# A Fourier mixing layer and windowed attention on one core: sums of v for six blocks a visit, T 19 blocks behind S

## The chip, the cores and the metric

The kernel runs on one core of one Trainium2 chip. A core has TensorE (PE in the profile; its weight loads are PEld), VectorE (DVE), ScalarE (ACT), GpSimd (POOL) and SyncE (SP), which here issues nearly all DMAs. The metric is the device time in microseconds of one execution; lower is better.

## The reference, cut to what matters

One input x of 2048 positions and 512 features goes through two branches, and a gate mixes them:

```
a = x @ Dre.T ; b = x @ Dim.T            # transform along the features
A = Cre @ a - Cim @ b                    # transform along the sequence, 2048 x 2048
q, k, v = x @ wqkv                       # 32 heads of 16
p = softmax(q k^T / 4), over the last 256 positions
B = (p v) @ wo
g = sigmoid(sum(x * gate_w))
out = g * A + (1 - g) * B
```

Products with float32 accuracy are made of three products of halves: each operand is split into a rounded high part (hi) and the rest (lo), and PE does hi hi, hi lo and lo hi.

## The kernel before, in words

**Two kinds of work side by side.** PE's order is written out by hand: the main loop at the end of the function issues, for each step n, the attention work of a few blocks and between them `fill(n)`, which takes the next matmuls out of a generator, `dense()`. The other engines' orders come from a scheduler that simulates times, with some instructions pinned behind others (`behind`, `late`). So a change in the loop can move instructions on every engine.

**Attention.** A block is 64 positions of one group of 8 heads, handled as four pairs p; there are 4 groups with 32 blocks, N = 128. Its way has two passes over the scores.
- S (`s_pair`, L355): the scores of a block as rows, four matmuls `s`. DVE adds the mask and takes the extreme of each row (L357), ACT the exponentials and their sum (L360). Eight blocks later `ml_split`, `ml_turn` and `ml_rows` turn these numbers into rows, which go through DRAM into four spare rows of `ring[0]` (`m_ring`, at n = 8u + 12).
- T (`t_pair`, L438): LAG = 18 blocks behind S, the scores again, transposed, with the m rows in the product. ACT writes the exponentials to `pt` (L439), POOL clears the corners (L444, L448). T of block 8u - 4 is the first that reads the m rows of u, because a block reaches 320 positions ahead.
- Sums of v (`pv`, L465): matmuls 32 columns wide, four beside each other on PE. They are done for several blocks in one go, a visit, once enough blocks have their exponentials: three blocks, and five when `more` isn't empty, that is, when the projections are through and only the sequence transform is left to fill in. The buffers for the exponentials are four of the pool, and from then on two more in `home`, a tile that held the outgoing projections.
- `o_out` (L486) multiplies a finished tile by the reciprocals of the sums and stores it to `o_scr`.

**Dense work.** `dense()` yields, in order: q, k and v of the first group (L270, L293), the other groups' q and k, the transform along the features (dab, L293), and then the sequence transform (dc, L517) in pieces: a piece is 128 x 1024 weights of Cre or Cim. Each is loaded to `raw` (two buffers, L94), split by DVE to hi and lo (L569, in `split_soon`: four jobs, taken at every sixth matmul), and used by 24 matmuls. `Pieces.get` takes a piece, starts the split of the next one and the load of the one after it. hi and lo come from a pool with three buffers each. `c_half` does half a sum of one output block; its accumulator r is loaded from `r_scr` when it starts and added when it is done (`ended`, taken at the second matmul of the next stretch).

**The end.** When the attention is through, `attention_done` loads wo through the same `raw` buffers and splits it (`fin`); for each output block, `wo_prep` loads o from `o_scr` and splits it on ACT and DVE (`os`, L78, L81), and `wo_block` multiplies (L777). These stand between the last pieces of dc.

**Queues.** SP issues in order; a DMA that waits holds all behind it. The last lines of `s_pair` and others record their instruction (`mark`), so that a pinned one can be put behind them.

Of the kernel before, what the change touches and what calls it, by code (L numbers as in the profile page):

```python
# [7 lines left out]
F32 = mybir.dt.float32  # L8
F32R = mybir.dt.float32r
AF = mybir.ActivationFunctionType  # L10
OP = mybir.AluOpType
# [11 lines left out]
WIN = 320  # L23
BIG = 1e30
SCALE = 0.25
LAG = 18
WARM = 8
SWITCH = 6
FILL_FIRST, FILL_PROJ, FILL_SEQ = 3.0, 4.0, 3.7
# [3 lines left out]
def fnet_window_mix(ctx: ExitStack, tc: tile.TileContext, xT, x, wqk, wv, wr, wi, cr, ci, wo, gw, out):  # L33
# [24 lines left out]
    def f(ap):  # L58
        return ap.bitcast(F32)
# [4 lines left out]
    def mark(e, ins):  # L64
        last[e] = ins.ins

    @contextmanager
    def behind(*engines):
        with ExitStack() as es:
            for e in engines:  # L70
                if e in last:
                    es.enter_context(tc.issue_after(last[e]))
            yield
# [15 lines left out]

    HALVES = slice(0, 512), slice(512, 1024)  # L90

    def load_raw(src):
        raw = st.tile([P, 1024], F32, name="raw", bufs=2)
        ld(raw, src)  # L94
        return raw

    def split_raw(raw, act=False):
        hi = st.tile([P, 1024], F32R, name="hi")
        lo = st.tile([P, 1024], F32R, name="lo")
        for c in HALVES:  # L100
            split(hi[:, c], lo[:, c], raw[:, c], act)
        return hi, lo
# [2 lines left out]
    ended = []  # L105

    def split_soon(raw):
        hi = st.tile([P, 1024], F32R, name="hi")
        lo = st.tile([P, 1024], F32R, name="lo")
        for c in HALVES:  # L110
            jobs.append(lambda c=c: late(nc.vector.tensor_copy, hi[:, c], raw[:, c]))
            jobs.append(lambda c=c: late(nc.vector.tensor_sub, lo[:, c], raw[:, c], f(hi[:, c])))
        return hi, lo
# [27 lines left out]

    with tc.manual_schedule(engines={mybir.EngineType.Activation, mybir.EngineType.DVE, mybir.EngineType.SP}):
        wraw, *xraw = [pt_raw() for _ in range(3)]
        wq0 = [st.tile([P, 1024], F32R, name=h) for h in ("hi", "lo")]
        zero = ev.tile([P, 512], F32R, name="ev")
        nc.vector.memset(f(zero[:]), 0.0)
        for dk in (0, 2, 1, 3):
            XRAW[dk, 0] = xraw[dk // 2][:, HALVES[dk % 2]]
            if dk % 2 == 0:
                nc.scalar.dma_start(XRAW[dk, 0], xT[0, dk])  # L150
        for dk in range(DK):
            ld(wraw[:, dk * 256:dk * 256 + 256], wqk[0][:, dk * 256:dk * 256 + 256])
            if dk % 2 == 0:
                ld(XRAW[dk + 1, 0], xT[0, dk + 1])
        for dk in range(DK):
            c = slice(dk * 256, dk * 256 + 256)
            mark("act", nc.scalar.copy(wq0[0][:, c], wraw[:, c]))
            split_x(0, (dk,), dk > 0)
            mark("dve", nc.vector.tensor_sub(wq0[1][:, c], wraw[:, c], f(wq0[0][:, c])))
# [27 lines left out]
                                        base=e - 1, channel_multiplier=-1)  # L187

    def clear_rows(i, ss):
        nc.gpsimd.memset(f(ring[i][96:128, :, ss * 512:(ss + 1) * 512]), 0.0)  # L190

    first_lo = f(XT[0, 0][96:128, 1]).rearrange("r (p c) -> r p c", p=NP)
    for t in pads[0]:
        nc.gpsimd.affine_select(t[96:128], first_lo, pattern=[[0, NP], [0, P]], compare_op=OP.is_gt, fill=0.0,
                                base=0, channel_multiplier=0)
    clear_rows(1, 0)
    clear_rows(0, 0)
    vpad = [const.tile([P, 4, NP, 32], F32, name=f"vpad{b}") for b in range(2)]
# [38 lines left out]
    TERMS = ((0, 0), (0, 1), (1, 0))  # L237


    home = const.tile([P, 3072], F32R, name="home")  # L240
    turn = iter(range(99))

    def hl_tile():
        c = next(turn) % 3 * 1024
        return home[:, c:c + 1024].rearrange("p (h s) -> p h s", h=2)

    def qk_evict(g, ss, i, ps):
        hl = hl_tile()
# [149 lines left out]
    OT = {}  # L398
    V2 = {}
    PT = {}  # L400
    more = []

    VR = {}
# [21 lines left out]
    def t_pair(n, p):  # L425
        q0 = n % NB * BQ
        w = min(WIN, S - q0)
        if p == 0:
            if "proj" in have:
                more.append(n)  # L430
            c = (n - more[0]) % 6 * NP * WIN if more else 3072
            if c + NP * WIN <= 3072:
                PT[n] = f(home[:, c:c + NP * WIN].rearrange("p (a b) -> p a b", a=NP))
            else:
                PT[n] = at.tile([P, NP, WIN], F32, name="pt", bufs=4)
        pt = PT[n]
        ps = ps_a.tile([P, 512], F32, name="t", tag="st")
        nc.tensor.matmul(ps[:, :w], PAD[1, n][:, p], ring[0][:, p, q0:q0 + w], start=True, stop=True)  # L438
        nc.scalar.activation(pt[:, p, :w], ps[:, :w], AF.Exp, scale=-1.0)  # L439
        if p % 2:  # L440
            ph = slice(p - 1, p + 1)
            for h in (0, 64):
                a = pt[h:h + 64, ph, 0:64]
                nc.gpsimd.affine_select(a, a, pattern=[[0, 2], [1, 64]], compare_op=OP.is_ge, fill=0.0,  # L444
                                        base=0, channel_multiplier=-1)
                if w == WIN:
                    a = pt[h:h + 64, ph, 256:320]
                    nc.gpsimd.affine_select(a, a, pattern=[[0, 2], [-1, 64]], compare_op=OP.is_gt, fill=0.0,  # L448
                                            base=0, channel_multiplier=1)
# [97 lines left out]
            dma.dma_start(out[15][:, c], r[:, c])  # L547
        yield

    def c_half(get, half, tb, j, ab, done, after=None):  # L550
        ps = ps_d.tile([P, 512], F32, name="dc", tag="d")
        w = get((half, tb * 2 + j))
        r = done[0](tb)
        for c in range(2):
            if after:
                after()
            k = 8 * j + 4 * c
            yield from c_part(w, range(16)[k:k + 4], ab, ps, (8 * j, 8 * j + 7))
            if c == 0:
                yield  # L560
        ended.append(lambda: late(done[1], tb, ps, r))
        yield
# [13 lines left out]
    def dense():  # L576
# [128 lines left out]
        for j in range(2):  # L705
            for tb in lasts:
                yield from c_half(pieces.get, 0, tb, j, ab,
                                  (lambda t: None, lambda t, ps, r: store_r(t, ps)) if j == 0 else
                                  add(lambda t: r_scr[0][t], lambda t: r_scr[2][t]),
                                  next_b if j else None)  # L710
        ab = nxt
        wait = []

# [16 lines left out]
        for j in range(2):  # L730
            for tb in first:
                yield from c_half(pieces.get, 1, tb, j, ab, add(r_in, lambda t: r_scr[2][t]) if j == 0 else
                                  add(lambda t: r_scr[2][t], lambda t: r_scr[1][t], wait.append),
                                  None if j else next_b)
        for tb in range(SWITCH, 16):
            if tb in O:
                mixed[tb] = wo_block(tb, 0)
            for w in [w for w in wait if w in O]:
                wait.remove(w)
                ld(out[w], wo_block(w, 1))  # L740
            if FIN and tb < 15:
                for w in (tb + 1, *wait[:-(-len(wait) // (15 - tb))]):
                    wo_prep(w)
            yield from c_block(pieces.get, 1, tb, ab, add_r) if tb < 15 else c_final(pieces.get, ab, mixed.pop(15))
# [82 lines left out]

    for n in range(N + LAG + 1):
        if n in (1, 3, 5):
            for i in range(2):  # L830
                clear_rows(1 - i, (n + 1) // 2)
        if n == 7:
            clear_pads()
        k = n - LAG
        ring_ahead(n + 1)
        if k in (-1, 4):
            v_spread(0 if k < 0 else 4)
        if k in (-4, -1, 4):
            v_next({-4: 0, -1: 4, 4: 8}[k])
        if n == 0:  # L840
            make_pad(0, 0)
        for p in range(NP):
            if n < N:
                s_pair(n, p)
            fill(n)
            if 0 <= k < N:
                t_pair(k, p)
            if p == 0:
                make_pad(0, n + 1)
                if k >= -1:  # L850
                    make_pad(1, k + 1)
            fill(n)
            for at_n, at_p, do in TURN:
                u, j = divmod(n - at_n, 8)
                if p == at_p and j == 0 and 0 <= u < 16:
                    do(u)
            if p == 3 and k % 8 == 6 and 0 <= k < N:
                l_load(k // 8)
            if p == 0 and full:
                o_out()  # L860
            if p == 2 and (k - summed >= (5 if more else 3) or k == N):
                for j in range(summed, k):
                    pv(j)
                summed = k
            if p == 3 and 4 * spread - 5 < summed and 4 * spread < N and n >= fresh:
                v_spread(4 * spread)
                spread += 1
                v_next(4 * spread)
                fresh = n + 2
# [49 lines left out]
```

## Time and profile before

| | |
|---|---|
| median of 3 runs | 859.54 us (859.01 to 862.26) |
| profiled execution | 859.55 us |
| its span, first to last instruction | 857.4 us |
| granted TensorE clock | 1.000 |
| DMA moved | 160.50 MB, mean 187 GB/s |
| POOL's selects on `pt` (L444, mean) | 357 ns |
| S exponentials on ACT (L360, mean) | 542 ns |
| S mask and extreme on DVE (L357, mean) | 463 ns |

The time of an execution is 2.15 us more than the span of its instructions. Matmuls overlap on PE: a 128 x 512 matmul is shown with 395 ns, while the next one starts about 230 ns after it; what one costs is read from start to start.

### The profile page before, as it was taken

What the parts mean: (1) busy time and instruction counts of PE and PEld (TensorE: products, weight loads), DVE (VectorE), ACT (ScalarE), POOL (GpSimd) and SP (SyncE); (2) the same over time, 40 slices, a digit from 0 to 9 for tenths busy, and PEclk for the clock granted to TensorE, in tenths of its full rate; (3) what the DMA queues carried; (4) which work ended last, traced back from release to release, by engine and by line L of the source; (5) the groups of instructions that cost most, each with busy time, mean ns of one, the idle gap of its engine ahead of it and who ended that gap; (6) DMA issues with size and microseconds to landing.
All of it is one profiled execution on the core that took longest, in us unless ns stands there. A gap on an engine that the chain in (4) does not pass through costs nothing.

```text
span 857.4 us, 17208 instructions
## 1 busy us (share of the span) xinstructions
PE 849.5 (99%) x5166; PEld 690.4 (81%) x5166; DVE 621.6 (72%) x2011; ACT 588.0 (69%) x1793; POOL 371.7 (43%) x1067
## 2 busy tenths in 40 slices
PE   9999999999999999999999999999999999999998
PEld 7888787887887888887788878888877888878887
DVE  5688977777978788777788777898878844455541
ACT  5488888888888888777888887786777654401110
POOL 9200344545533545555545564553456666510000
PEclk9999999999999999999999999999999999999999
DMA  7876678484857173536264546897963544247652
GB/s 252 287 221 202 193 255 260 164 283 167 253 184 215 37 228 116 161 116 166 90 175 130 152 135 210 262 284 247 253 205 120 200 149 142 99 147 247 209 172 98
DMA packets 94573, 160.50 MB, mean 187 GB/s; under 512 B 27280, under 2 KB 36240, under 8 KB 94480
## 3 DMA queue, kind: packets, MB, share of 16 engines
q1 hardware_dynamic: 94048, 158.76, 59.3%
q8 instruction: 40, 0.66, 0.3%
q10 hardware_dynamic: 432, 0.66, 0.2%
q14 instruction: 53, 0.43, 0.2%
HBM read 108.00 MB, written 51.38 MB: 186 GB/s over the span
## 4 chain that ended last, share of the span: by engine, by line
PE 96%; DVE 2%; DMA 1%; issue 0%; ACT 0%; SPq 0%; DVEq 0%
PE dc L517 40%; PE dab L293 10%; PE s L355 9%; PE dqk L270 9%; PE t L438 8%; PE o L465 8%; PE dv L293 5%; PE t L777 5%; DMA ring<-m_scr 1%; PE s L258 1%; DVE sm L357 1%; DVE pad L338 0%; DMA pt<-xT 0%; DVE lo L569 0%; PE s L375 0%
## 5 line engine op out<-in xcount | busy, mean ns | idle before, releaser
L517 PE MATMUL dc<-big,hi 128*128 128x512 f32 x1020 | 350.3, 395 | 0.0
L360 ACT ACTIVATE sm<-sm,ml 128x320 f32<-128x320 f32 (+4 forms) x512 | 277.1, 542 | 92.1 <-DVE ml L357 87.0
L357 DVE CUSTOM_DVE_ANT_0 sm<-s,mask 128x320 f32<-128x320 f32 (+4 forms) x512 | 234.7, 463 | 106.3 <-PE s L355 78.5
L444 POOL TENSOR_SCALAR_AFFINE_SELECT pt<-pt 64x128 f32<-64x128 f32 x392 | 140.1, 357 | 222.6 <-ACT pt L439 211.9
L517 PEld LDWEIGHTS dc<-big,hi 128*128 128x128 f32 x1020 | 183.3, 188 | 26.7 <-issue 1.1
L517 PE MATMUL dc<-big,lo 128*128 128x512 f32 x510 | 201.4, 395 | 0.0
L439 ACT ACTIVATE pt<-t 128x320 f32<-128x320 f32 (+4 forms) x392 | 160.6, 410 | 48.5 <-PE t L438 46.0
L355 PE MATMUL s<-ring,pad 128*128 128x320 f32 (+4 forms) x512 | 158.6, 310 | 0.6 <-DVE ml L357 0.4
L438 PE MATMUL t<-ring,pad 128*128 128x320 f32 (+4 forms) x512 | 154.6, 302 | 1.8 <-DMA ring<-m_scr 1.6
L338 DVE TENSOR_SCALAR pad<-ring,half 96x256 fp32r<-96x256 f32 x384 | 120.0, 360 | 19.0 <-PE t L438 18.6
L355 PEld LDWEIGHTS s<-ring,pad 128*128 128x128 f32 x512 | 96.1, 188 | 34.0 <-issue 9.5
L448 POOL TENSOR_SCALAR_AFFINE_SELECT pt<-pt 64x128 f32<-64x128 f32 x344 | 116.1, 337 | 0.0
L438 PEld LDWEIGHTS t<-ring,pad 128*128 128x128 f32 x512 | 96.1, 188 | 23.8 <-ACT sm L360 2.0
L517 PEld LDWEIGHTS dc<-big,lo 128*128 128x128 f32 x510 | 95.9, 188 | 13.4 <-issue 0.5
L569 DVE TENSOR_TENSOR lo<-raw,hi 128x512 fp32r<-128x512 f32 x142 | 97.9, 699 | 0.0
L360 ACT ACTIVATION_READ_ACCUMULATOR sm<-sm,ml 128x1 f32 x512 | 97.4, 190 | 0.0
L293 PE MATMUL dab<-hi,big 128*128 128x512 f32 x256 | 89.2, 394 | 0.0
L270 PE MATMUL dqk<-big,hi 128*128 128x512 f32 x240 | 84.9, 393 | 0.0
L569 DVE CAST hi<-raw 128x512 fp32r<-128x512 f32 x142 | 61.9, 447 | 16.9 <-PE dc L517 15.8
L444 POOL TENSOR_SCALAR_AFFINE_SELECT home<-home 64x128 f32<-64x128 f32 x120 | 45.7, 381 | 61.4 <-ACT home L439 54.2
L422 POOL COPY vpad<-vr 64x256 f32<-64x256 f32 x64 | 26.5, 414 | 103.4 <-DMA vr<-v_scr 74.2
L336 ACT ACTIVATE pad<-ring,half 96x256 fp32r<-96x256 f32 x128 | 63.8, 499 | 0.0
(96 smaller groups left out, 958.3 us busy)
## 6 DMA issues: line engine op xcount, KB each, us to landing
qk_scr<-home SPq DMA_DIRECT2D x32, 512.0 KB
ring<-qk_scr SPq DMA_DIRECT2D x32, 512.0 KB
raw<-cr SPq DMA_DIRECT2D x32, 512.0 KB
raw<-ci SPq DMA_DIRECT2D x32, 512.0 KB
r_scr<-ev SPq DMA_DIRECT2D x41, 256.0 KB
ev<-r_scr SPq DMA_DIRECT2D x41, 256.0 KB
ab_scr<-home SPq DMA_DIRECT2D x20, 512.0 KB
big<-ab_scr SPq DMA_DIRECT2D x20, 512.0 KB
```

The source lines that it names most:

```text
L270: nc.tensor.matmul(ps, w[a][:, c:c + 128], XT[dk, ss][:, b], start=n == 0, stop=n == 11)
L293: nc.tensor.matmul(ps, XT[dk, ss][:, a, c * 128:(c + 1) * 128], wh[b], start=n == 0, stop=n == 11)
L338: nc.vector.tensor_scalar(dst, src, half[:96, h:h + 1], None, op0=OP.mult)
L355: nc.tensor.matmul(ps[:, :w], PAD[0, n][:, p], ring[1][:, p, k0:k0 + w], start=True, stop=True)
L357: mark("dve", nc.vector.tensor_tensor_reduce(out=sm[:, :w], in0=ps[:, :w], in1=mask[:, WIN - w:], scale=1.0, scalar=3e38, op0=OP.add, op1= ...
L360: mark("act", nc.scalar.activation(sm[:, :w], sm[:, :w], AF.Exp, bias=nm[:, c], scale=-1.0, accum_out=l[:, c]))
L438: nc.tensor.matmul(ps[:, :w], PAD[1, n][:, p], ring[0][:, p, q0:q0 + w], start=True, stop=True)
L439: nc.scalar.activation(pt[:, p, :w], ps[:, :w], AF.Exp, scale=-1.0)
L444: nc.gpsimd.affine_select(a, a, pattern=[[0, 2], [1, 64]], compare_op=OP.is_ge, fill=0.0, base=0, channel_multiplier=-1)
L448: nc.gpsimd.affine_select(a, a, pattern=[[0, 2], [-1, 64]], compare_op=OP.is_gt, fill=0.0, base=0, channel_multiplier=1)
L517: nc.tensor.matmul(ps, w[a][:, i % 8 * 128:i % 8 * 128 + 128], ab[SC[i]][:, b], start=i == ends[0] and a + b == 0, stop=i == ends[1] and a ...
L569: return fn(*args)
```

## The change: what it does

- **Visits.** With `more`, the sums wait for six blocks instead of five, and stop at an even block.
- **Buffers of exponentials.** Eight instead of six from then on: four of the pool, four in a new view of `home`, which grows from 3072 to 5120 columns.
- **Weights.** hi and lo no longer come from a pool of three. There are three fixed pairs; the first lies in the first 2048 columns of `home`, and the order of use is written out. The first ten weights go round the three pairs as before; all later ones, the pieces of the sequence transform, use the other two in turn. That frees the columns of `home` for exponentials.
- **LAG** is 19.
- **Accumulators.** `c_half` may load r for the following half in the middle of its own (`ahead`).
- **The end.** Once `FIN` is set, ended sums are added ahead of the next block's output products.
- POOL's clears of the ring rows are pinned behind its first selects.

The diff, cut to its core:

```
-LAG = 18
+LAG = 19
...
+    home = const.tile([P, 5120], F32R, name="home")
+    slots = iter([0, 1, 2] * 3 + [0] + [1, 2] * 32)
+    hls = [[const.tile([P, 1024], F32R, name=f"{h}{i}") for h in ("hi", "lo")] for i in range(2)]
+    hls.insert(0, [home[:, c] for c in (slice(0, 1024), slice(1024, 2048))])
+
+    def wslot():
+        return hls[next(slots)]
...
     def split_soon(raw):
-        hi = st.tile([P, 1024], F32R, name="hi")
-        lo = st.tile([P, 1024], F32R, name="lo")
+        hi, lo = wslot()
...
-        nc.gpsimd.memset(f(ring[i][96:128, :, ss * 512:(ss + 1) * 512]), 0.0)
+        with behind("pool"):
+            nc.gpsimd.memset(f(ring[i][96:128, :, ss * 512:(ss + 1) * 512]), 0.0)
...
-        return home[:, c:c + 1024].rearrange("p (h s) -> p h s", h=2)
+        return home[:, 2048 + c:3072 + c].rearrange("p (h s) -> p h s", h=2)
...
-            c = (n - more[0]) % 6 * NP * WIN if more else 3072
-            if c + NP * WIN <= 3072:
-                PT[n] = f(home[:, c:c + NP * WIN].rearrange("p (a b) -> p a b", a=NP))
+            if len(more) == 1:
+                PTS.append(const.tile([P, 4, NP, WIN], F32, name="pts", tag="home"))
+            c = (n - more[0]) % 8 if more else 4
+            if c < 4:
+                PT[n] = PTS[0][:, c]
...
-    def c_half(get, half, tb, j, ab, done, after=None):
+    def c_half(get, half, tb, j, ab, done, after=None, after_tb=None):
...
-        r = done[0](tb)
+        r = ahead.pop(0) if ahead else done[0](tb)
...
             if c == 0:
+                if after_tb is not None:
+                    ahead.append(done[0](after_tb))
                 yield
...
         for tb in range(SWITCH, 16):
+            if FIN:
+                while ended:
+                    ended.pop(0)()
...
-            if p == 2 and (k - summed >= (5 if more else 3) or k == N):
-                for j in range(summed, k):
+            if p == 2 and (k - summed >= (6 if more else 3) or k == N):
+                end = k - k % 2 if more else k
+                for j in range(summed, end):
                     pv(j)
-                summed = k
+                summed = end
```

More of the change, by code (lines that the diff above doesn't have):

```diff
@@ L107, in split_soon @@
     def split_soon(raw):
-        hi = st.tile([P, 1024], F32R, name="hi")
-        lo = st.tile([P, 1024], F32R, name="lo")
+        hi, lo = wslot()
         for c in HALVES:
@@ L143, in fnet_window_mix @@
         wraw, *xraw = [pt_raw() for _ in range(3)]
-        wq0 = [st.tile([P, 1024], F32R, name=h) for h in ("hi", "lo")]
+        wq0 = wslot()
         zero = ev.tile([P, 512], F32R, name="ev")
@@ L189, in clear_rows @@
     def clear_rows(i, ss):
-        nc.gpsimd.memset(f(ring[i][96:128, :, ss * 512:(ss + 1) * 512]), 0.0)
+        with behind("pool"):
+            nc.gpsimd.memset(f(ring[i][96:128, :, ss * 512:(ss + 1) * 512]), 0.0)
     first_lo = f(XT[0, 0][96:128, 1]).rearrange("r (p c) -> r p c", p=NP)
     for t in pads[0]:
-        nc.gpsimd.affine_select(t[96:128], first_lo, pattern=[[0, NP], [0, P]], compare_op=OP.is_gt, fill=0.0,
-                                base=0, channel_multiplier=0)
+        mark("pool", nc.gpsimd.affine_select(t[96:128], first_lo, pattern=[[0, NP], [0, P]], compare_op=OP.is_gt,
+                                             fill=0.0, base=0, channel_multiplier=0))
     clear_rows(1, 0)
@@ L237, in fnet_window_mix @@
     TERMS = ((0, 0), (0, 1), (1, 0))
-    home = const.tile([P, 3072], F32R, name="home")
     turn = iter(range(99))
@@ L400, in fnet_window_mix @@
     PT = {}
+    PTS = []
     more = []
@@ L548, in c_final @@
         yield
-    def c_half(get, half, tb, j, ab, done, after=None):
+    ahead = []
+    def c_half(get, half, tb, j, ab, done, after=None, after_tb=None):
         ps = ps_d.tile([P, 512], F32, name="dc", tag="d")
         w = get((half, tb * 2 + j))
-        r = done[0](tb)
+        r = ahead.pop(0) if ahead else done[0](tb)
         for c in range(2):
@@ L709, in dense @@
                                   add(lambda t: r_scr[0][t], lambda t: r_scr[2][t]),
-                                  next_b if j else None)
+                                  next_b if j else None, tb + 1 if j and tb < 15 else None)
         ab = nxt
@@ L733, in dense @@
                                   add(lambda t: r_scr[2][t], lambda t: r_scr[1][t], wait.append),
-                                  None if j else next_b)
+                                  None if j else next_b, tb + 1 if tb + 1 < SWITCH else None)
         for tb in range(SWITCH, 16):
+            if FIN:
+                while ended:
+                    ended.pop(0)()
             if tb in O:
```

## The prediction

> **What bounds the kernel now.** I read the page first, then who waited for whom on PE, then the chain that ended last.
>
> ```profile
> span 857.4 us, 17208 instructions
> ...
> PE 849.5 (99%) x5166; PEld 690.4 (81%) x5166; DVE 621.6 (72%) x2011; ACT 588.0 (69%) x1793; POOL 371.7 (43%) x1067
> ...
> PE 96%; DVE 2%; DMA 1%; issue 0%; ACT 0%; SPq 0%; DVEq 0%
> ```
>
> PE is busy for 99% of the span and holds 96% of the chain. Its work isn't changed: the same matmuls run in another order. So only three things can move the time: what PE waits for, what it loses between matmuls of different kinds, and new waits.
>
> ```profile
> PE t L438 <- DMA ring<-m_scr: 1.6, 1, 1.6
> PE dv L574 <- DVE ev L146: 1.5, 1, 1.5
> PE s L258 <- DVE big L80: 0.5, 1, 0.5
> PE s L355 <- DVE ml L357: 0.4, 2, 0.2
> ```
>
> These are all of PE's waits: 4.0 us. The second and third are the start, which the change leaves alone. The first is a single stall of 1.6 us, a T matmul that waits for the m rows.
>
> **Sums of v: three visits fewer.** The chain in order of time has each visit of L465 as one row: start, length, count of matmuls.
>
> ```profile
> 163.08 1.75 PE o L465 x24
> ...
> 552.35 2.84 PE o L465 x56
> ...
> 791.21 10.88 PE dc L517 x48
> ```
>
> The first row is a visit of three whole blocks, the second one of five. A block costs (2.84 - 1.75) / 2 = 0.545 us, so 1.75 - 3 x 0.545 = 0.115 us of a visit belongs to no block. The third row gives a dc matmul alone: 10.88 / 48 = 0.227 us. Around the second visit the timeline of PE has more:
>
> ```profile
> 551.57 0.31 PE L438 MATMUL t<-ring,pad 128*128 128x320 f32 x1
> 551.72 0.63 PE L517 MATMUL dc<-big,hi 128*128 128x512 f32 x2
> 552.28 1.28 PE L465 MATMUL o<-home,vpad 128*32 128x320 f32 x16
> 553.38 1.81 PE L465 MATMUL o<-pt,vpad 128*32 128x320 f32 x40
> 555.12 0.41 PE L355 MATMUL s<-ring,pad 128*128 128x320 f32 x1
> 555.37 0.39 PE L517 MATMUL dc<-big,lo 128*128 128x512 f32 x1
> ```
>
> Two dc matmuls at 0.23 would end at 552.18, and L465 starts at 552.28: 0.10 us lost on the way in. On the way out the s matmul takes 0.25 us to the next start (555.12 to 555.37), where the t matmul ahead of the visit took 0.15 (551.57 to 551.72): 0.10 lost again. A visit so costs 0.10 + 0.115 + 0.10 = 0.32 us beside its blocks.
>
> Visits before: 12 of three blocks up to block 36, 18 of five up to 126, one of two: 31. After: 12, 15 of six, one of two: 28; the instruction order of the changed kernel has these 28. The gain is 3 x 0.32 = **0.96 us**. A six-block visit lasts about 0.115 + 6 x 0.545 = 3.4 us. No new wait lies in it: its last block's exponentials are used some 5 x 0.545 = 2.7 us after it begins. The even limit keeps the end of one output tile and the first use of the tile after next out of one visit, so o_out always gets in between.
>
> **T one block later: the stall on the m rows.** The stall, and the issue of the load:
>
> ```profile
> 617.18 0.66 SPq L56 DMA_DIRECT2D ring<-m_scr  x1
> ...
> 621.79 0.63 PE L517 MATMUL dc<-big,hi 128*128 128x512 f32 x2
> ...
> 624.04 0.39 PE L438 MATMUL t<-ring,pad 128*128 128x320 f32 x1 [1.62 <-DMA ring<-m_scr]
> ```
>
> Two dc matmuls and then t should be 0.46 us apart; they are 2.25: **1.79 us** lost. The rows came 6.9 us after their issue. With LAG 19 this T block stands one block later while m_ring keeps its place at block 8u + 12. How long is a block?
>
> ```profile
> 529.40:552.30 22.90, 22.90 (x118) 19.43 (x117) 21.16 (x70) 19.76 (x62) 13.46 (x40) 1.00 0.64 212
> ...
> 634.50:658.10 23.60, 23.54 (x121) 19.59 (x124) 22.33 (x76) 20.03 (x64) 14.39 (x40) 1.00 0.46 155
> ```
>
> These are windows between two visits, five blocks each (length; then PE, PEld, DVE, ACT, POOL busy). A block is 4.6 us. The rows were 1.8 us late and get 4.6 us more, so I count the whole 1.79 as gained. In the new order the load of v for a later group stands directly ahead of this m load on SP's queue, and it waits for POOL; that wait would have to cost 2.8 us more than before. Kept ends: 0 and 1.79.
>
> **Weights in two slots instead of three.** Each split then waits for the matmuls of the piece before. While S runs, the split is issued after the third matmul of the next piece, when those are done: no wait is added, and in the new order no split has a wait on PE of its own until S has ended. After that DVE does stand for PE. Behind it stand the pads of T, and each still has over 4 us of PE work between that release and its first use. I count nothing; the work that covers it is DVE's slack, 23.60 - 22.33 = 1.3 us in the fullest window above, and if that goes PE stands. The run between visits is now six blocks at the same load, so the short s waits (0.4 us above) may grow or go: ends -1 and +1 us, taken as 0, the nearest row. The earlier ev loads, the fixed order of POOL's clears and the eight buffers get nothing: no row above has PE waiting for any of them.
>
> **The end: the first output product comes sooner.** The loop has one block more, so it uses 11 more dc matmuls, and they are missing as cover behind the last sums.
>
> ```profile
> 762.39 0.54 PE L465 MATMUL o<-pt,vpad 128*32 128x128 f32 x16
> 762.86 0.74 PE L517 MATMUL dc<-big,hi 128*128 128x512 f32 x2
> ...
> 777.32 4.97 PE L777 MATMUL t<-fin,os 128*128 128x512 f32 x21
> ```
> ```profile
> 754.04 8.59 SPq L56 DMA_DIRECT2D raw<-wo  x2
> 763.51 0.33 SPq L56 DMA_DIRECT2D raw<-ci  x1
> 764.12 0.33 SPq L56 DMA_DIRECT2D o_scr<-ev  x1
> ...
> 769.33 2.58 SPq L56 DMA_DIRECT2D ev<-o_scr  x5
> ```
> ```profile
> 763.41 0.68 DVE L486 TENSOR_TENSOR ev<-o,ev 128x512 f32<-128x512 f32 x1
> 765.91 0.76 DVE L80 CAST fin<-raw 128x512 fp32r<-128x512 f32 x2 [1.82 <-DMA raw<-wo]
> 766.59 1.29 DVE L81 TENSOR_TENSOR fin<-raw,fin 128x512 fp32r<-128x512 f32 x2
> 768.74 0.76 DVE L569 CAST hi<-raw 128x512 fp32r<-128x512 f32 x2 [0.86 <-DMA raw<-ci]
> ...
> 773.36 0.69 DVE L81 TENSOR_TENSOR os<-ev,os 128x512 fp32r<-128x512 f32 x1 [2.66 <-ACT os L78]
> ```
> ```profile
> 772.71 0.62 ACT L78 CAST os<-ev 128x512 fp32r<-128x512 f32 x1 [13.03 <-DMA ev<-o_scr]
> ```
>
> Let v be the end of the last sums (762.86). Before, L777 came at v + 14.5 and its first os was whole at v + 11.2 (774.05). In the new order 52 dc matmuls stand there: PE arrives at v + 52 x 0.227 = v + 11.8.
>
> The chain is longer now. The first wo load waits for a split that waits for the end of a piece on PE. Behind that end stand 12 dc matmuls and three narrow t (2.9 us) and the visit (762.39 to 762.86, 0.47), so it lies at v - 3.4; with a subtraction of 0.7 and SP's step the load goes out at v - 2.5. A load of this size took 3.6 us (the second wo: issued in the last 0.33 us before 754.04 + 8.59 = 762.63, used at 765.91): v + 1.1. Fin's first half, 2.0 us (765.91 to 767.88): v + 3.1. L486, which now stands behind it on DVE, 0.7: v + 3.8; store of o, 0.1 later. The store took 5.2 us (764.12 to 769.33) behind two such loads; behind one I take 4.2: v + 8.1. Load of o, 3.4 (769.33 to 772.71): v + 11.5. ACT and DVE, 1.35 (772.71 to 774.05): v + 12.85. The first two matmuls of L777 (0.45 us) don't need DVE's half. So PE stands 12.85 - 0.45 - 11.8 = **0.6 us**. With 5.2 us for the first load and for the store it is 3.2; with none of DVE's new order in the way, 0.
>
> The Trainium skill (DMA: Bandwidth & Descriptors, "Anatomy of one DMA") fits a DMA by 2.0 us plus its bytes at 436 GB/s, measured on another issue path; 256 KB would be 2.6 us by it, an estimate. By that rule the store and the load of o save 2.4 us, the stall is gone and the sum is 856.8. The trace has 5.2 and 3.4, and I go by these.
>
> **Sum.** The profiled execution took 859.55 us, against a median of 859.54. 859.55 - 0.96 - 1.79 + 0.6 = **857.4 us**.
>
> **Rivals.**
> - *The m rows are late again.* The v load ahead of them holds SP, and the stall stays: 859.55 - 0.96 + 0.6 = 859.2. For it: two vr loads stood near that m load before as well. Against it: 4.6 us more room. Chance 0.12.
> - *Slower: the end.* Fin, then the product, then the store, all behind a late wo load: 3.2 us instead of 0.6, which gives 860.0. It decides from 2.75 us on, when both gains are spent. For it: a ci load took 5.2 us (763.51 to 768.74). Against it: one large load fewer ahead of the store. Chance 0.12.
> - *Slower by more: DVE.* With 95% busy in the fullest window, a wait of 0.2 us on the slot in each of some 40 pieces beside S would come through to PE: 857.4 + 8 = 865. Against it: the order puts the split behind the release. Chance 0.08.
> - *Faster: short stalls go too.* The gaps too short for the list of waits shrink by some 2 us, as DVE's bursts and T's fall on other blocks, and the end costs nothing: 854.8. Chance 0.08.
> - *Buffers were the bubble.* Each visit's 0.32 us would be a wait for a free buffer, and eight buffers end it: 859.55 - 31 x 0.32 - 1.79 + 0.6 = 848.4. Against it: the loss is the same for visits of three and five, and PE's list has no such wait. Chance 0.03. The Trainium skill (Perfetto Trace Analysis, "Optimization Strategy") says that a gap that repeats on the saturated engine can mean too few buffers; the rows here don't bear that out.
>
> That the visits don't become larger is excluded by the order of the instructions.
>
> **How the numbers follow.** The forecast has the remaining 0.57. It and the first two rivals (0.81 together) give the range: down to 859.55 - 2.75 - 1 with a little for scatter, 855.0; up to 860.0 plus 1 us of s waits, 861.3 with scatter. Half a per cent is 4.3 us, about what a measurement of this kernel can tell from no change. Faster by more: the last two rivals, 0.11. Slower by more: DVE, 0.08. Within: 0.81.
>
> **What would show it.** Right: 28 runs of the sums on PE, six blocks in about 3.4 us; no wait of t for the m rows; at the first output product a wait of PE for os of under 1.5 us. Wrong: a wait of that kind over 2.7 us; s matmuls that wait for DVE in sum over 2 us; a split of weights beside S that waits for dc; an in-visit loss that isn't near 0.32.

## The result and the profile after

The changed kernel takes **863.66 us** (median of 16 runs, 862.57 to 866.16) against 860.06 for the kernel before in the same series: a ratio of 1.0041 (95% interval 1.0028 to 1.0054). It is slower by 3.6 us; I had forecast 2.1 us less. The profiled execution has a span of 861.7 us, 4.3 more than before. These are the lines of its page that answer to those of before:

```profile
span 861.7 us, 17211 instructions
...
PE 853.9 (99%) x5166; PEld 692.0 (80%) x5166; DVE 620.8 (72%) x2011; ACT 588.6 (68%) x1793; POOL 372.7 (43%) x1067
...
PE 95%; DVE 2%; DMA 2%; issue 1%; ACT 1%; SPq 0%; DVEq 0%; ACTq 0%
```

PE has the same 5166 matmuls and is busy 4.4 us longer (853.9 against 849.5). All of the loss is in there. The list of PE's waits (total, times, longest) has nothing of that size:

```profile
PE dv L587 <- DVE ev L152: 1.5, 1, 1.5
PE s L361 <- DVE ml L363: 1.3, 3, 0.9
PE s L264 <- DVE big L80: 0.4, 1, 0.4
PE t L447 <- DVE mhl L392: 0.4, 1, 0.4
PE s L264 <- DVE big L81: 0.3, 1, 0.3
PE s L361 <- ACT pts L448: 0.3, 1, 0.3
```

In sum it is 4.2 us against 4.0. The wait for the m rows is gone, as forecast, and none for the output products has come; in its place s waits 1.3 us for DVE, which was 0.4. The chain in order of time (start, length) shows what the list can't:

```profile
550.20 3.38 PE o L474 x64
...
795.23 10.99 PE dc L526 x48
```

The first is a visit of six blocks, 3.38 us long as forecast (3.4). The second is the row that stood at 791.21 before, 48 dc matmuls and nothing between them: 10.99 us instead of 10.88. The work is the same and PE waits for nothing, and each matmul takes 0.229 us instead of 0.227. Only 2.3 ns, but there are 3,758 matmuls outside the sums.

So I took the start times of all matmuls from both traces and split the time from each start to the next: 0.4427 ns per column (226.7 ns for 512) as the ideal; up to 60 ns above it as loss of spacing; more than that as a stall; the visits of the sums by themselves (their ideal is a quarter of 0.4427 ns per column, as four stand beside each other).

| us | before | after | difference |
|---|---|---|---|
| ideal | 748.8 | 748.8 | 0 |
| loss of spacing | 15.55 | 20.38 | **+4.82** |
| stalls over 60 ns, the m rows | 1.79 | 0 | -1.79 |
| other stalls over 60 ns | 13.84 | 15.82 | +1.98 |
| visits, over their ideal | 38.36 | 37.66 | -0.70 |

The sum is +4.3, the difference of the spans. The table tells how the time is divided, not why. Of the 4.82 us, 3.0 stand where a long matmul is followed by a short s or t (2.71 us before, 5.73 after, at some 990 places), 1.3 between two long ones (dv, dqk and dab; from dc to dc it went from 4.46 to 4.21), 0.5 behind short ones. So the row of dc matmuls is a sign of the loss and not where most of it stands. The granted clock is 1.00 in both profiles. What also changed are addresses: the 36 KB of `home` and the weight pairs now lie first in SBUF, and everything else has moved.

### The profile page after: what moved, and what is told of

The parts are those of the page before. It is cut to its first block, busy times and chain, and to the rows that moved or that the text cites. A ratio compares the mean times of both kernels' runs of the same rounds, so it can differ in the third digit from the quotient of the medians.

```text
span 861.7 us, 17211 instructions
## 1 busy us (share of the span) xinstructions
PE 853.9 (99%) x5166; PEld 692.0 (80%) x5166; DVE 620.8 (72%) x2011; ACT 588.6 (68%) x1793; POOL 372.7 (43%) x1067
## 4 chain that ended last, share of the span: by engine, by line
PE 95%; DVE 2%; DMA 2%; issue 1%; ACT 1%; SPq 0%; DVEq 0%; ACTq 0%
PE dc L526 40%; PE dab L299 10%; PE dqk L276 9%; PE s L361 9%; PE o L474 8%; PE t L447 8%; PE dv L299 5%; PE t L793 5%; DMA qk_scr<-home 1%; DMA pt<-wqk 1%; DVE pad L344 1%; PE s L264 0%; DVE sm L363 0%; PE s L381 0%; DVE lo L582 0%
## 5 line engine op out<-in xcount | busy, mean ns | idle before, releaser
L453 POOL TENSOR_SCALAR_AFFINE_SELECT pt<-pt 64x128 f32<-64x128 f32 x332 | 119.4, 360 | 196.5 <-ACT pt L448 184.4
L448 ACT ACTIVATE pt<-t 128x320 f32<-128x320 f32 (+4 forms) x332 | 135.1, 409 | 37.7 <-PE t L447 35.2
L453 POOL TENSOR_SCALAR_AFFINE_SELECT pts<-pts 64x128 f32<-64x128 f32 x180 | 69.8, 388 | 83.3 <-ACT pts L448 76.4
L366 ACT ACTIVATION_READ_ACCUMULATOR sm<-sm,ml 128x1 f32 x512 | 97.6, 191 | 0.0
L448 ACT ACTIVATE pts<-t 128x320 f32<-128x320 f32 (+1 forms) x180 | 74.0, 413 | 32.9 <-PE t L447 28.8
L582 DVE TENSOR_TENSOR lo<-raw,hi 128x512 fp32r<-128x512 f32 x136 | 94.4, 696 | 1.8
L457 POOL TENSOR_SCALAR_AFFINE_SELECT pt<-pt 64x128 f32<-64x128 f32 x280 | 93.8, 335 | 0.0
L582 DVE CAST hi<-raw 128x512 fp32r<-128x512 f32 x136 | 59.6, 440 | 31.4 <-PE dc L526 27.9
L276 PE MATMUL dqk<-big,home 128*128 128x512 f32 x264 | 76.8, 396 | 0.0
L299 PE MATMUL dab<-hi,big 128*128 128x512 f32 x192 | 70.3, 398 | 0.1
```

Source lines behind the costliest of these rows:

```text
L276: nc.tensor.matmul(ps, w[a][:, c:c + 128], XT[dk, ss][:, b], start=n == 0, stop=n == 11)
L299: nc.tensor.matmul(ps, XT[dk, ss][:, a, c * 128:(c + 1) * 128], wh[b], start=n == 0, stop=n == 11)
L366: mark("act", nc.scalar.activation(sm[:, :w], sm[:, :w], AF.Exp, bias=nm[:, c], scale=-1.0, accum_out=l[:, c]))
L582: return fn(*args)
```

## The experiments

Theory **place**: where the operands lie in SBUF sets the spacing. Rival **order**: the new order of work, the two slots and the waits cost the 3.6 us. Addresses below are bytes per partition, as the compiled kernels have them.

**e1: a map of places.** A kernel of matmuls alone.

> This kernel computes none of the reference: 45 tiles of 4 KB per partition fill SBUF with zeros, and TensorE alone runs 128x512 matmuls with the weights and the moving data at chosen pairs of tiles (a grid of 12 x 12 places, 8 matmuls each, then finer steps, then the hi-hi, hi-lo, lo-hi pattern of the sequence transform). Nothing else runs beside them. Theory 'place' (the spacing of matmuls depends on where the two operands lie in SBUF): the mean spacing differs from cell to cell, from about 226 ns to 229, 232 or more, and is constant within a cell. Rival 'order' (the extra 4.8 us between matmuls of the changed kernel comes from its order of work and its waits): every cell has the same spacing, 226.5 ns within 0.5. If place holds, the grid also tells which relation counts: weights below the moving data, or one of the operands in the low part of SBUF.

All 144 cells of the grid, from 1 KB to 181 KB for either operand, have 226.6 or 226.7 ns. So "low" and "high" mean nothing by themselves. But 71 of the 72 cells with finer steps had means of 230 to 234 ns, at every place alike, with a pattern set by the steps' size. They have only eight matmuls each, so the change from cell to cell is in them too (see e9). Place held in another form than I had it: the region doesn't count, and the low bits of the addresses were the next suspect.

**e2 to e4: the same instructions at other places.** The order on every engine is that of the kernel they come from; only the order of the pools differs. e2:

```
 big = tile_pool("big", bufs=16)
+wt = tile_pool("wt", bufs=1)
-home = const.tile([P, 5120] ...)      # the pairs and pts likewise
+home = wt.tile([P, 5120] ...)
```

> The changed kernel with the same instructions in the same order on every engine; only the pool of the weights (home and the two pairs) is opened behind that of the 16 big tiles, so that the pairs lie at 167104 to 183487 as they did before, above the moving data, and pads and rings lie where they did before. Theory 'place': the spacing in the quiet end goes from about 229 back to 226.5 ns, the small excess between matmuls from 20.4 to about 15.5 us, and the time from 863.7 to about 858.8 us (span near 857), a little under the kernel before. Rival 'order': nothing changes, 863.7 us, 229 ns.

In e3 `wt` is opened between const and big:

> As the run before it, but the weights lie between the rings and the big tiles (pairs at 101568 to 117951, big at 117952 to 183487 as in the changed kernel). Theory 'place' with 'weights below the moving data' as the relation: as slow as the changed kernel, 863.7 us, 229 ns in the quiet end. Theory 'place' with 'an operand in the low 80 KB' as the relation: about 858.8 us, 226.5 ns. Rival 'order': 863.7 us.

In e4, the kernel before, hi and lo come from a pool opened ahead of const:

> The kernel before with the same instructions in the same order on every engine; only the pool of the three pairs of weights is opened first, so that they lie at 1152 to 25727, and everything that lay below them moves up by 24576 bytes. Theory 'place': about 4.8 us slower, near 864.9 us, with 229 ns in the quiet end. Rival 'order': 860.1 us as before, 226.5 ns.

e2: **858.62 us**, ratio to before 0.9974 (0.9961 to 0.9987). e3: **858.82**, 0.9978 (0.9967 to 0.9989). e4: **864.30**, 1.0047 (1.0029 to 1.0064). The rows of 48 dc matmuls, in the chains of e2, e3 and e4:

```profile
792.31 10.88 PE dc L526 x48
```
```profile
790.77 10.88 PE dc L526 x48
```
```profile
795.08 10.99 PE dc L517 x48
```

The rival falls: with not one instruction moved, the changed kernel gains 5 us, and the kernel before loses 4. The loss of spacing goes with it: 15.27, 14.73 and 19.28 us. e3 also rules out "weights below the moving data".

**e5: which bits.** In the compiled addresses the weights and the big tiles differ by a multiple of 128 bytes before and in e2 and e3, and by an odd multiple of 64 after and in e4.

> This kernel computes none of the reference: TensorE alone runs cells of 40 matmuls of 128x512 (zeros), each cell with one offset of the weights and one of the moving data within their tiles (0, 32, 64, 96, 128 bytes each, then some of 8 and 16, then cells whose matmuls alternate between two pairs of offsets, then 128x320); both tiles begin at a multiple of 128 bytes. Theory 'halves' (a matmul is slow where its weights and its moving data begin in different 64-byte halves of a 128-byte unit): 226.7 ns where both offsets are 0, both 64 or 128 against 0; about 229 ns in the mean where one is 0 and the other 64. Rival 'low' (an operand in the low part of SBUF makes it slow): all cells alike, since all lie at 1 to 9 KB. Rival 'odd starts' (any start that is no multiple of 128 bytes costs by itself): 64 against 64 is slow too.

Windows of 32 spacings each (length, then busy times of PE and PEld; the counts include matmuls cut by the edges; the 1.00 behind them is the granted clock), with weights and moving data at 0 and 0, 0 and 64, 0 and 128, 64 and 0, 64 and 64:

```profile
15.71:22.97 7.26, 7.26 (x34) 6.01 (x32) 0.00 (x0) 0.00 (x0) 1.00 0.01 2
34.14:41.47 7.33, 7.33 (x34) 6.01 (x32) 0.00 (x0) 0.00 (x0) 1.00 0.00 0
52.66:60.13 7.47, 7.47 (x34) 6.01 (x32) 0.00 (x0) 0.00 (x0) 1.00 0.00 0
108.24:115.71 7.47, 7.47 (x34) 5.98 (x32) 0.00 (x0) 0.00 (x0) 1.00 0.01 2
126.88:134.13 7.25, 7.25 (x34) 6.01 (x32) 0.00 (x0) 0.00 (x0) 1.00 0.00 0
```

Equal offsets give 226.7 ns, at 32, 96 and 128 too; moving data 64 above the weights 229.0; every other pair of multiples of 32 gives 232 to 234 (0 and 128: 233.3; 128 and 0: 232.1). "Odd starts" falls for 32 to 96 bytes (8 and 8, or 16 and 16, were slow at 233). "Halves" is half right: 0 against 128 isn't fast. 128x320 matmuls had 146.7 ns in all four pairs of 0 and 64.

**e6 to e8: 64 bytes moved.** The edit of e6 and e7:

```
+gp = tile_pool("gp", bufs=1)          # behind big
-e = const.tile([P, 16], F32, name="ge")
+e = gp.tile([P, 16], F32, name="ge")
```

> The changed kernel, the same instructions in the same order; a 64-byte tile that lay in front of the 16 big tiles (the gate's temporary) is put behind them, so that the big tiles begin 64 bytes lower and everything else stays: the weights at 1152 to 38015, low as in the changed kernel. Theory 'halves': weights and big tiles now begin in the same 64-byte half: 226.6 ns in the quiet end, small excess 15.5 us or less, 857 to 859 us. Rival 'low': as the changed kernel, 863.7 us and 229 ns.

> The kernel before, the same instructions in the same order, with the same edit: the 64-byte tile goes from in front of the big tiles to behind them, so that the big tiles begin 64 bytes lower, and the weights stay at 158912 to 183487, high. Theory 'halves': weights and big tiles now begin in different 64-byte halves: 229 ns in the quiet end, small excess near 20 us, about 864.5 us. Rival 'low': nothing changes, 860.3 us.

> As e6, and the output weights begin at the start of their tile instead of 64 bytes into it, so that they lie in the same 64-byte half as the attention output that is multiplied with them. Theory 'halves': the three spacings of the 192 output products go from 229.0, 231.7 and 226.0 ns to 226.7 each, 0.44 us in all, less than the times can resolve; so e6's time within 1 us, and the spacing in the trace decides. Rivals: no change of spacing.

e7: **866.50 us**, 1.0064 (1.0042 to 1.0087), 5.9 us slower by 64 bytes alone. Its row has 11.20 us, 233.3 ns each, which is what e5 has for moving data 64 below the weights:

```profile
799.11 11.20 PE dc L517 x48
```

"Low" falls with that. But e6 wasn't fast: **864.47**, 1.0040 (1.0021 to 1.0060), where I expected 857 to 859. e8 took **863.92**, 1.0038 (1.0020 to 1.0055). At the quiet end they do what halves said. The rows of e6 and e8:

```profile
798.39 10.93 PE dc L526 x48
```
```profile
796.26 10.88 PE dc L526 x48
```

In e6 the first ten spacings, behind the output products, are 224 to 236 ns, and all the rest 226.7; in e8 all are 226.7. There the output products are at 227.0, 226.0 and 227.0 ns (229.0, 231.7 and 226.0 before and after; 0.43 us in all). While S and T run, the loss grew: from a dc matmul to a short s or t 5.9 to 6.8 ns in the mean, against 2.8 to 3.5 in e2, and between two dab matmuls 8.4 against 4.9. In sum the loss of spacing was 20.98 and 20.54 us. So neighbours of different kinds count too.

**e9: the period, and a mix.**

> This kernel computes none of the reference: TensorE alone runs zeros. First cells of 40 equal 128x512 matmuls with the weights at one offset and the moving data at 0, 64, ... 512 bytes from it; then 64 cells that copy the mix of the kernels (two 128x512 matmuls in the hi-hi, hi-lo, lo-hi order between short ones of 128x320), in which pads and rings are shifted by 0 to 448 bytes each against the long matmuls' operands. Theory 'phase modulo 512' (what counts is the difference of the two operands' start addresses modulo 512 bytes): 0 and 512 give 226.7 ns, 64 gives 229.0, the others 232 to 234. If 256 is as fast as 0, the period is 256. For the mixed cells it forecasts that the mean loss per matmul depends on the two shifts, that pads and rings shifted by 448 (64 bytes below the long operands, as in the kernel before) lose less than pads and rings shifted by 0 (as in e6), and by how much the best cell would beat both. Rival: mixed cells all lose the same, and e6 was slow for another reason.

Windows of 32 spacings with the moving data 0, 64, 128, 192 and 256 bytes above the weights:

```profile
16.05:23.31 7.26, 7.26 (x34) 6.01 (x33) 0.00 (x0) 0.00 (x0) 1.00 0.01 2
25.15:32.48 7.33, 7.33 (x33) 6.01 (x32) 0.00 (x0) 0.00 (x0) 1.00 0.00 0
34.34:41.77 7.43, 7.43 (x34) 6.03 (x32) 0.00 (x0) 0.00 (x0) 1.00 0.00 0
43.64:51.11 7.47, 7.47 (x33) 6.02 (x32) 0.00 (x0) 0.00 (x0) 1.00 0.00 0
52.96:60.22 7.26, 7.26 (x34) 6.01 (x32) 0.00 (x0) 0.00 (x0) 1.00 0.00 0
```

For a pair that doesn't change the period is **256 bytes**: 226.7, 228.8, 232.1, 233.4 ns, and again. The cells at 256 and 512 first take ten spacings of 224 to 236 ns, as e6 did, and only then stay at 226.7: a new pair has to settle. While S and T run (100 to 700 us), mostly two and never more than four long matmuls stand between two short ones, too few to settle; that this is why the mix loses more isn't shown. The start addresses modulo 256 sort the quiet ends of these kernels (pads and rings at 128 in each):

| kernel | weights | big tiles | dc alone, ns | by e9, ns |
|---|---|---|---|---|
| before, e2, e3 | 192 | 192 | 226.7 | 226.7 |
| after | 128 | 192 | 229.0 | 228.8 |
| e4 | 128 | 192 | 229.0 | 228.8 |
| e7 | 192 | 128 | 233.3 | 233.4 |
| e6, e8 | 128 | 128 | 227.7, 226.7 | 226.7 |

In the mixed cells the loss per matmul runs from 1.6 to 8.0 ns with the two shifts. The cells that I had named beforehand come out the wrong way round: the shifts of e6 lose 3.9 there, those of before 6.1. But with the rings 256 bytes further, the same shift modulo 256, the cell of e6 loses 8.0 and that of before 1.9, so these cells don't tell which kernel is the faster.

**e10 and e11: T 18 or 19 blocks behind S.** One number each, LAG 18 in e3 and LAG 19 in the kernel before.

> e3 (the changed kernel with weights between rings and big tiles) with T 18 blocks behind S again. The prediction's step on the m rows: the 1.79 us wait of T for them at the one group comes back, so 860.6 us against e3's 858.8. Rival: the wait was hidden by work that came later anyway, so 858.8 us.

> The kernel before with T 19 blocks behind S and nothing else changed: visits, buffers, weights and their places stay. The prediction's step on the m rows: 860.4 - 1.79 = 858.6 us, with no wait of T for the m rows. Rival: the m rows are late again behind the load of v, 860.4 us. Theory 'phase': since S and T read the rings at steps of 256 bytes, one block of lag more shifts T against S by 256 bytes, and the small excess may move by some tenths of a us.

e10: **857.46 us**, 0.9965 (0.9947 to 0.9982). e11: **860.85**, 1.0003 (0.9988 to 1.0018). Neither forecast fits e10: its wait for the m rows came back, and it is still no slower than e3. e11 has the rival's time, but not its reason. With LAG 19 the wait for the m rows goes, and no time is gained. In e11 the stalls over 60 ns grow from 15.63 to 16.43 us although the 1.79 are gone from them. The largest, 1.11 us, ends with the s matmul at 97.6 us; in the changed kernel it is this one, 1.07 us, first on PE, then on DVE in the stretch before:

```profile
98.88 0.41 PE L361 MATMUL s<-ring,pad 128*128 128x320 f32 x1 [0.90 <-DVE ml L363]
```
```profile
97.58 0.40 DVE L390 TENSOR_SCALAR mhl<-s 32x256 fp32r<-32x256 f32 x1
98.01 0.28 DVE L391 COPY mhl<-s 32x128 f32<-32x128 f32 x1
98.33 0.49 DVE L363 CUSTOM_DVE_ANT_0 sm<-s,mask 128x320 f32<-128x320 f32 x1
```

The evictions for the m rows stand ahead of the reduction that frees the PSUM tile for s. The kernel before has the same order on DVE, from 96.51 us, and its s matmuls there lose 0.23 and 0.39 us. So this place adds some 0.45 us, and the order on DVE alone doesn't explain it.

**e12 and e13: pads and rings moved.** Both start from e10, with the output weights as in e8. In e12 two of the gate's 64-byte tiles go in front of the pads and two between pads and rings; in e13 three go in front of the pads. The edit of e12, cut:

```
+gl = const.tile(...); g1 = const.tile(...)
 pads = [[const.tile(...
+g0 = const.tile(...); ge = const.tile(...)
 ring = [const.tile(...
```

> e10 (the changed kernel, weights between rings and big tiles, T 18 behind S) with the same work; four 64-byte tiles go from behind the rings to the front of pads and rings, so that modulo 256 bytes the pads begin 64 bytes and the rings 192 (or, by the rings' steps, 448) bytes past the long operands, where both began 64 bytes below them; the output weights begin at the start of their tile, as in e8. Theory 'phase' with the mixed cells of e9 taken as they are (1.6 to 2.1 ns lost per matmul against 1.9 to 6.1): the small excess goes from 14.9 to 6 to 9 us, the time to 849 to 852 us. Rival 'phase, but the mix of e9 is not that of the kernel' (e6 did not follow it): the long matmuls and the output products at the quiet end stay at 226.7 ns, and the small excess lands anywhere between 12 and 22 us. Rival 'S and T do not matter': 14.5 us and 857 us.

> As e12, but three of these tiles go in front of the pads, so that pads and rings begin 128 bytes past the long operands modulo 256 (2.8 to 2.9 ns lost per matmul in e9's cells, whichever step the rings are at). Theory 'phase' with e9's cells: small excess 9 to 11 us, time 852 to 854 us. Rivals as for e12: anywhere between 12 and 22 us, or 14.5 us and 857 us.

e12: **853.66 us**, 0.9922 (0.9901 to 0.9944), the fastest here: 6.8 us below the kernel before, 10.0 us below the changed one. Modulo 256 its pads begin at 0 instead of 128, and the rings stay at 128. The loss of spacing is 10.32 us, against 14.95 in e10: between dc matmuls 2.9 ns in the mean (4.6), from dc to s 1.0 (3.2). It won this although its wait for the m rows was longer than ever:

```profile
PE t L447 <- DMA ring<-m_scr: 2.5, 1, 2.5
```

e13 took **857.94**, 0.9970 (0.9955 to 0.9985), with 15.43 us lost in spacing; the cell of e9 had forecast 9 to 11. So the short matmuls' offsets count, "S and T do not matter" falls, and e9's mix isn't a guide to size: e12 came out above its 6 to 9 us, e13 far above.

## Why the prediction was wrong, step by step

- **"Its work isn't changed ... So only three things can move the time": the step that failed.** The same matmuls at other addresses aren't the same work. Moving the weights in front of everything put them 64 bytes out of step with the big tiles modulo 256, and the spacing lost 4.82 us more, which no term held. Of the three things, "what it loses between matmuls of different kinds" was priced at the visits alone; 3.0 of the 4.82 us came where short matmuls follow long ones. e2, e3, e4 and e7 show the loss come and go with the places, without a moved instruction. The offset between weights and big tiles isn't all of it, as e6 shows: it took this offset away and kept the loss. Of what I read beforehand the row of 48 dc matmuls had it: 226.7 ns each there, while the output products at the end of the same profile were at 229, 232 and 226 ns. That difference had no explanation, and I passed over it. With the weights elsewhere the change comes near the forecast in number: e2 and e3 are 1.5 to 1.7 us below the kernel before, and the forecast was 2.1 below its profiled run. In part that is luck, because the largest term, the m rows, didn't hold as a gain.
- **Visits: right.** There are 28, the six-block ones take 3.38 us, and -0.70 us is found on the way in and within them. The way out, 0.11 us each before and after, stands in the other stalls and brings -0.30 more: -1.00 against the -0.96 of the forecast.
- **The m rows: right as a stall, wrong as a gain.** The 1.79 us went. The prediction says "I count the whole 1.79 as gained". The short waits, which I held at 0 with ends of -1 and +1, grew by 1.98, or by 2.28 without the ways out of the visits, and e11 shows LAG 19 alone to gain nothing. Some 0.45 us of that stand at the rows at 97.6 us; what makes the others, of 0.4 to 0.6 us each, stays open.
- **Weights in two slots: right.** No wait of PE for them is in the list.
- **The end: no stall where I had 0.6 us.** The first product starts 12.0 us after the last sums (769.32 to 781.33), against v + 11.8 in the working, and waits for nothing:

```profile
781.11 0.39 PE L526 MATMUL dc<-big,lo 128*128 128x512 f32 x1
781.33 0.62 PE L793 MATMUL t<-fin,os 128*128 128x512 f32 x2
```

- **The rivals:** of the slower ones the end didn't come, and of DVE's load there is 1.3 us of s waits against 0.4 before, not 8. That its 865 lies near the 863.66 is chance. What did come, addresses, wasn't among them.

The Trainium skill (SBUF — State Buffer, "Who interferes with whom") gives PE two independent read ports, one for the moving operand and one for the weights, and says that PE never waits on anyone. No run here shows ports; but the spacing does depend on how the two operands lie to each other, with nothing else running (e5, e9). What in the chip does it stays open, and so does a rule for the mixed order of long and short matmuls: e6 and e8 didn't follow the pairs, and e12 and e13 not the size of the mix. Not tried: e12 with LAG 19, and the other shifts of pads and rings.

## What to carry to other kernels

A change that adds, drops or moves a tile moves all tiles behind it, so compare the start addresses of matmul operands modulo 256 bytes before and after, and take the time of one long run of equal matmuls from each profile, without its first ten: if it differs and nothing waits in it, look at the addresses ahead of the schedule. Where PE is the bound, try a few 64-byte shifts of the operands before reworking the order, and measure each one, as neither pairs nor the mix forecast them; here the best one brought 3.8 us (e12 against e10), more than the change itself was to bring. When a stall is moved, price the waits that the same shift makes elsewhere, not only the one that goes.

## What the runs showed of the hardware

- The spacing of 128x512 matmuls of 4-byte data, one pair of operands again and again, settles at 226.7 ns when the moving data and the weights start at the same address modulo 256 bytes, 228.8 with the moving data 64 above, 232.1 with 128 (233.3 in e5), 233.4 with 192 (e9); 32 or 96 bytes apart it is 233 to 234 (e5). Cells with starts that are only multiples of 8 or 16 bytes were at 230.6 to 233.5, the two with equal starts at 233. The region of SBUF doesn't count (e1: 1 to 181 KB, 226.6 or 226.7 ns).
- Behind matmuls of another pair, matmuls at equal starts took up to ten spacings of 224 to 236 ns before they were at 226.7 (e9 at 256 and 512 bytes, e6 behind the output products).
- A cell that alternates two pairs which are fast by themselves (0 and 0, 64 and 64) has 231.7 ns (e5): what counts is also how one matmul's operands lie to the next one's.
- In this kernel 10 to 22 us of 860 are lost in spacing. By tile offsets alone, in an unchanged order, it was 15.6 to 22.2 us in the order of before (before, e4, e7), 14.7 to 21.0 in that of after (e2, e3, e6, e8), 10.3 to 15.4 in that of e10 (e12, e13). Some of it may stay at any offset: 128x320 matmuls alone took 146.7 ns in all four pairs tried, 5 more than the ideal.
